# A spectral filter and a SoLU block on one core: the opening reordered, with buffers in the free half of y, idle products and conversions shared by three engines

## The chip, the core and the metric

The kernel runs on one core of a Trainium2 chip. The metric is the device time of one execution, in microseconds (us). A core has a tensor engine (PE, with its weight loads shown apart as PEld), VectorE (DVE), ScalarE (ACT), GpSimd (POOL) and SyncE (SP), which only issues transfers here. The engines run their own instruction streams and meet through semaphores. The on-chip memory is SBUF, with 128 partitions; products of PE land in PSUM.

## The reference

```python
# x (8, 3136, 256), filt_r and filt_i (1569, 256)
X = np.fft.rfft(x, axis=1)
Y = X * (filt_r + 1j * filt_i)[None]
t = np.fft.irfft(Y, n=3136, axis=1).reshape(25088, 256)
h = t @ w_in                                   # (256, 1024)
e = np.exp(h - max(h)); sm = e / (sum(e) + 1e-9)
solu = h * sm
ln = (solu - mean(solu)) / sqrt(var(solu) + 1e-6) * g_ln
out = ln @ w_out                               # (1024, 256)
```

The two weights come as 64-bit floats[...]: the kernel turns their bit patterns into 32-bit floats itself.

## The kernel before

**Two parts.** A main loop over 196 blocks of 128 tokens, taken in 98 pairs, runs the SoLU block and, interleaved with it by a table of due times (`PLAN`), the spectral filter of batches 1 to 7. Batch 0 has to be filtered before the loop can begin; this is the opening, the `with ExitStack() as st:` block from L305 on, whose order is written by hand. At its end the pools of the opening are closed and those of the main loop opened, over the same SBUF.

**The filter of one batch** is a Fourier transform in three steps. `first` (L204) multiplies pieces of x with a table (`pa`, L210), ACT copies the result to `t` (tile `t1`, L212), and it is stored to the DRAM buffer d1. x has 8 pieces of 4 columns, each with two halves of 49 rows. After all of d1 is written, 7 units (`self.units`, the last half as large) follow: `fetch` reads a unit's rows of d1 into `t2` (in the trace `t<-d`, L228), `forward` multiplies with a table `de` (`pb`, L238), `multiply` forms the complex product with the filter `f` on DVE in five operations and on POOL in one (L259 to L261), `inverse` multiplies back (`pc`) and ACT copies to `g` (L276), and `store` (L280) writes to d2. Last, `fetch_back` reads d2 into `t4` (L166, L167), and `back` makes the last products (`py`, L298), which ACT copies to `y` (L301).

**y** holds the tokens of two batches; in the opening the half of batch 1 is free and is filled at the end with six x pieces of batch 1 (`fetch_second`, L352).

**The other work of the opening:** the eight weight pieces are loaded as 32-bit words (`begin`, `load_words`, tile `raw`) and converted on DVE in ten operations of 128x512 (`load_float64`, L326 to L340); `weight_sums` forms sums of the converted w_in; tables `de` and filters `f` are loaded in two groups (units 0 and 1; the rest) by POOL, L357 and L360; the filters are copied to `f_dram` (L448) for the later batches. Ten products with an unused result (`idle`, L441) run ahead of the back transform.

**Queues.** A transfer is issued by the engine whose queue it uses, in that engine's order: SP's issues wait in front of each other, and so do POOL's and ACT's between their computations. Batch 0's fetches are on SP, the stores of `g` on POOL, the stores of `t1` on ACT (96 rows) and SP (4 rows). Completion is counted by eight semaphores for SP and ACT together and eight for POOL; a new transfer takes the next one in turn and waits until its last user has landed.

**Overlaps in SBUF.** A tile of the main loop that lies over a tile of the opening waits for that tile's last use: `h`, the first tile that the loop writes, lies over the filters `f` and so waits for their copy to f_dram.

The line numbers of the prediction and the profile before are those printed here.

Of the kernel before, what the change touches and what calls it, by code (L numbers as in the profile page):

```python
# [17 lines left out]
P = 128  # L18
# [11 lines left out]
NCH = 4  # L30
# [58 lines left out]
def kernel(  # L89
# [79 lines left out]
    class Spectrum:  # L169
# [34 lines left out]
        def first(self, i, halves, ps, evac):  # L204

            n0, n = 2 * halves[0], 2 * len(halves)
            self.t1s[i, n0] = t1 = self.pools["t1"].tile([NK, n, C], FP32,
                                                         name=f"t1_{self.e}_{i}_{n0}", tag="t1")
            for j, u in enumerate(halves):
                nc.tensor.matmul(out=ps[0:NK, j], lhsT=wf_t, rhs=self.xs[i][0:NR, 2 * u:2 * u + 2, :],  # L210
                                 start=True, stop=True)
            evac(out=t1.rearrange("p n c -> p (n c)"), in_=ps[0:NK].rearrange("p a b -> p (a b)"))  # L212
# [12 lines left out]
        def fetch(self, i, dma):  # L225
            self.t2s[i] = self.buffer(i, "t2", [P, 4, C])
            rows, n = self.rows(i, d1[self.e])
            dma(out=self.t2s[i][:, 0:n, :], in_=rows)  # L228
# [55 lines left out]
    def fetch_back(e, ch, rows_pool, split=None):  # L284

        split = split or whole
        t4s[e, ch] = rows_pool.tile([P, NCH, C], FP32, name=f"t4_{e}_{ch}", tag="r")[0:NK]
        split(
            (nc.sync.dma_start if split is by_16 else nc.gpsimd.dma_start, nc.sync.dma_start), t4s[e, ch],
            d2[e].rearrange("s (a n) c -> (s a) n c", a=4)[:, NCH * ch:NCH * ch + NCH, :])  # L290
# [14 lines left out]
    with ExitStack() as st:  # L305
        pools = {name: pool(name + "0", bufs, stack=st)
                 for name, bufs in (("r", 8), ("t1", 4), ("t2", 2), ("p", 2), ("g", 2))}
        fpool = pool("fp", 1, stack=st)
# [10 lines left out]
        def load_float64(dst, raw, negate=False):  # L319


            lo, hi = raw[:, :, 0], raw[:, :, 1]
            power = wpool.tile([P, 512], I32, name="power", tag="power", bufs=1)
            frac = dst.bitcast(I32)
            ts, stt = nc.vector.tensor_scalar, nc.vector.scalar_tensor_tensor
            ts(out=power, in0=hi, scalar1=20, scalar2=0x7FF, op0=ALU.logical_shift_right,  # L326
               op1=ALU.bitwise_and)
            ts(out=power, in0=power, scalar1=896.0, scalar2=0.0, op0=ALU.subtract, op1=ALU.max)
            ts(out=power, in0=power, scalar1=255.0, scalar2=None, op0=ALU.min)
            ts(out=power, in0=power, scalar1=23, scalar2=-2 ** 31 if negate else 0,  # L330
               op0=ALU.logical_shift_left, op1=ALU.bitwise_or)
            stt(out=power, in0=hi, scalar=-2 ** 31, in1=power, op0=ALU.bitwise_and,
                op1=ALU.bitwise_xor)
            ts(out=frac, in0=hi, scalar1=0xFFFFF, scalar2=3, op0=ALU.bitwise_and,
               op1=ALU.logical_shift_left)
            nc.vector.tensor_tensor(out=frac, in0=frac, in1=power, op=ALU.bitwise_or)
            ts(out=lo, in0=lo, scalar1=8, scalar2=None, op0=ALU.logical_shift_right)
            rest = power.bitcast(FP32)
            stt(out=rest, in0=lo, scalar=2.0 ** -44, in1=rest, op0=ALU.mult, op1=ALU.mult)
            nc.vector.tensor_tensor(out=dst, in0=dst, in1=rest, op=ALU.add)  # L340
# [7 lines left out]

        def fetch_second():
            for i in range(6):  # L350
                out = spare[i % 2][:, i // 2 * NCH * C:(i // 2 + 1) * NCH * C]
                second.fetch_x(i, [lambda out, in_: nc.sync.dma_start(out=out, in_=in_)] * 2,  # L352
                               out.rearrange("p (n c) -> p n c", c=C))

        def load_tables(i0, n):
            de = fpool.tile([P, n, 2, 2, NQ], FP32, name=f"de_{i0}", tag=f"de{i0}")
            nc.gpsimd.dma_start(out=de, in_=de_dram[i0:i0 + n].rearrange("i p k u q -> p i (k u q)"))  # L357
            f = fpool.tile([P, n, 2, C], FP32, name=f"f_{i0}", tag=f"f{i0}")
            for place, k, held, rows in all_filter_rows(i0, n):
                nc.gpsimd.dma_start(out=f[place, 0:held, k, :], in_=rows)  # L360
# [31 lines left out]
        def fetch_x(i):  # L392
            sp.fetch_x(i, (lambda out, in_: by_16((nc.sync.dma_start, nc.sync.dma_start), out, in_),
                           lambda out, in_: nc.gpsimd.dma_start(out=out, in_=in_)))
# [3 lines left out]
        pieces = NH // NCH  # L398
        for i in range(pieces):
            fetch_x(i)  # L400
            if i == 5:
                begin(0)
        begin(1)
        load_tables(0, 4)
        begin(2)
        for i in range(pieces):
            sp.first(i, (0, 1), ps_h.tile([P, 2, 512], FP32, name=f"pa_0_{i}", tag="h"),
                     nc.scalar.copy)
            sp.store_first(i, 0, lambda out, in_: by_16((nc.scalar.dma_start, nc.sync.dma_start), out, in_))
        for j in range(4):  # L410
            load_float64(weights[j][0], raws.pop(j), negate=True)
            if j == 0:
                begin(3)
                load_tables(4, NP - 4)
        nc.gpsimd.dma_start(out=wi_t, in_=wi_dram)
        nc.gpsimd.dma_start(out=g_sb, in_=moe_g_ln.rearrange("(k p) -> p k", p=P))
        weight_sums(w_in_sb)
# [6 lines left out]
        units = len(sp.units)  # L424
        for i in range(2):
            sp.fetch(i, nc.sync.dma_start)
            start(i)
        for i in range(units):
            if i + 2 < units:
                sp.fetch(i + 2, nc.sync.dma_start)  # L430
                start(i + 2)
            sp.multiply(i, 0, nc.vector.tensor_tensor)
            sp.multiply(i, 1, nc.gpsimd.tensor_tensor)
            sp.inverse(i, [ps_t.tile([P, 2, C], FP32, name=f"pc_0_{i}_{u}", tag="t") for u in range(2)])
            sp.store(i, nc.gpsimd.dma_start)
            if i in (2, 3, 4):
                begin(i + 2)

        for j in range(10):
            idle = ps_h.tile([P, 2, 512], FP32, name=f"idle_{j}", tag="h")  # L440
            nc.tensor.matmul(out=idle[:, 0, :], lhsT=tables[0][0][:, 0, 0].rearrange("p u q -> p (u q)"),  # L441
                             rhs=filters[0][0][:, 0].rearrange("p k c -> p (k c)"), start=True, stop=True)
        for ch in range(pieces):
            fetch_back(0, ch, pools["r"], by_16)
        fetch_second()
        for i0, n, rows in ((0, 4, P), (4, NP - 5, P), (NP - 1, 1, NQ)):
# [4 lines left out]
        for ch in range(pieces):  # L451
            for cb in range(KD):
                back(0, ch, cb, nc.scalar.copy)
        for j in range(4, 8):
            load_float64(weights[j][0], raws.pop(j))
            if j == 4:
                begin(7)
# [12 lines left out]

    wk = pool("wk", 1)
    wk2 = pool("wk2", 2)
    upool = pool("up", 2)
    spool = pool("sp", 1)
    rs_dram = pool("rs_dram", 2, DRAM)
    hpool = pool("hp", 2)
    pools = {name: pool(name + "1", bufs)
             for name, bufs in (("r", 3), ("t1", 3), ("t2", 1), ("p", 1), ("g", 1))}
    pools.update(f=pool("fp1", 2), de=pool("de1", 2))
# [74 lines left out]
    def pair_sums(j):  # L554

        s14 = wk2.tile([P, 2, P], FP32, name=f"s14_{j}", tag="s14")
# [352 lines left out]
```

## Time and profile before

| What | Value |
|---|---|
| Time | 1733.19 us, median of 3 runs (1730.2 to 1734.39) |
| Span of the profiled execution | 1733.2 us, 30221 instructions |
| PE busy | 1624.6 us, 94% |
| DVE, ACT, POOL busy | 71%, 54%, 63% |
| Moved by DMA | 308.71 MB, mean 178 GB/s |
| First `pb` on PE | 56.46 us |
| First `py` on PE | 107.52 us |
| First `h` on ACT | 137.84 us |

The page of a profile lists each engine's busy time, the span in 40 slices, the transfer queues, the chain of work that ended last, and groups of instructions by source line. The trace also answers for a stretch of time: a table of windows with each engine's busy time, the clock that was granted to PE, the busy share of the DMA engines and the rate; a timeline, in which equal neighbours are merged (x2); and the list of who waited for whom. `DMA_DIRECT2D` on SPq, ACTq or POOL is only the issue of a transfer, not the transfer. An engine's time in a row is that of the merged group.

### The profile page before, as it was taken

What the parts mean: (1) busy time and instruction counts of PE and PEld (TensorE: products, weight loads), DVE (VectorE), ACT (ScalarE), POOL (GpSimd) and SP (SyncE); (2) the same over time, 40 slices, a digit from 0 to 9 for tenths busy, and PEclk for the clock granted to TensorE, in tenths of its full rate; (3) what the DMA queues carried; (4) which work ended last, traced back from release to release, by engine and by line L of the source; (5) the groups of instructions that cost most, each with busy time, mean ns of one, the idle gap of its engine ahead of it and who ended that gap; (6) DMA issues with size and microseconds to landing.
All of it is one profiled execution on the core that took longest, in us unless ns stands there. A gap on an engine that the chain in (4) does not pass through costs nothing.

```text
span 1733.2 us, 30221 instructions
## 1 busy us (share of the span) xinstructions
PE 1624.6 (94%) x9792; PEld 1118.7 (65%) x9792; DVE 1225.5 (71%) x2599; ACT 939.9 (54%) x1726; POOL 1087.7 (63%) x1310
## 2 busy tenths in 40 slices
PE   4487899899999999999999999999999999999996
PEld 1352356676666667676667666766777777777776
DVE  4552877667777777678776778668777777777772
ACT  2133455546655555665566455664556566656551
POOL 4214687457666576667676666757656666567673
PEclk7688899999999999999999999999999999999999
DMA  9675788766786688658765676567754454444443
GB/s 276 188 225 182 225 246 254 200 183 167 222 243 203 170 229 237 167 153 222 233 181 139 190 220 198 154 155 210 216 139 102 119 121 120 113 105 103 112 109 92
DMA packets 363247, 308.71 MB, mean 178 GB/s; under 512 B 63425, under 2 KB 327642, under 8 KB 363090
## 3 DMA queue, kind: packets, MB, share of 16 engines
q1 hardware_dynamic: 285906, 146.01, 33.3%
q0 software_dynamic: 43984, 126.02, 24.5%
q10 hardware_dynamic: 33200, 34.74, 6.8%
q8 instruction: 80, 1.31, 0.3%
q14 instruction: 77, 0.63, 0.1%
HBM read 122.34 MB, written 81.50 MB: 118 GB/s over the span
## 4 chain that ended last, share of the span: by engine, by line
PE 71%; DMA 8%; DVE 7%; issue 3%; ACT 2%; POOL 2%; SPq 1%; ACTq 0%; POOLq 0%; DVEq 0%
PE o L686 29%; PE m L574 28%; PE py L298 5%; PE pa L210 4%; DVE h L622 3%; DMA solu_t<-turn 3%; PE pb L238 2%; PE pc L238 2%; DMA t<-d 2%; DMA de<-de_tbl 1%; ACT e L606 1%; DMA f_dram<-f 1%; DMA out_dram<-ot 1%; DVE h L595 1%; SPq L644 1%
## 5 line engine op out<-in xcount | busy, mean ns | idle before, releaser
L624 ACT ACTIVATE e<-h,nmu 128x1024 f32<-128x1024 f32 x196 | 225.3, 1150 | 338.3 <-DVE h L622 334.0
L686 PE MATMUL o<-w_out_sb,solu_t 128*128 128x128 f32 x3136 | 404.0, 277 | 4.7 <-DVE rsum L617 2.1
L686 PEld LDWEIGHTS o<-w_out_sb,solu_t 128*128 128x128 f32 x3136 | 381.6, 194 | 36.7 <-issue 29.0
L686 PEld LDWEIGHTS o<-w_out_sb,u 128*128 128x128 f32 x2352 | 307.4, 192 | 145.0 <-issue 113.3
L574 PE MATMUL m<-w_in_sb,s 128*128 128x512 f32 x784 | 397.9, 599 | 1.0 <-ACT h L584 1.0
L686 PE MATMUL o<-w_out_sb,u 128*128 128x128 f32 x2352 | 313.4, 276 | 6.4 <-ACT ot L698 5.7
L552 POOL TENSOR_TENSOR u<-solu_t 128x512 f32<-128x512 f32 x98 | 150.1, 1532 | 268.2 <-DMA solu_t<-turn 136.4
L574 PE MATMUL m<-w_in_sb,y 128*128 128x512 f32 x588 | 307.5, 606 | 7.8 <-DVE nmax L598 4.6
L622 DVE SCALAR_TENSOR_TENSOR h<-e,rsum,h 128x1024 f32<-128x1024 f32 x196 | 283.7, 1447 | 7.0
L705 DVE SCALAR_TENSOR_TENSOR ot<-o,rs_t,ot 128x128 f32<-128x128 f32 x294 | 102.6, 349 | 249.4 <-ACT ot L698 203.3
L584 ACT COPY h<-m 128x512 f32<-128x512 f32 x294 | 172.5, 587 | 132.8 <-PE m L574 113.6
L632 DVE STREAM_TRANSPOSE turn<-h 128x1024 f32<-128x1024 f32 x196 | 242.5, 1237 | 1.6 <-DVE ot L705 0.4
L598 DVE CUSTOM_DVE_ANT_0 h<-m,h 128x512 f32<-128x512 f32 x196 | 134.5, 686 | 135.4 <-ACT h L584 105.9
L606 ACT ACTIVATE e<-h,nmax 128x1024 f32<-128x1024 f32 x196 | 225.0, 1148 | 0.0
L552 POOL TENSOR_TENSOR u<-solu_t,u 128x512 f32<-128x512 f32 x98 | 139.0, 1418 | 96.6 <-PE o L686 92.7
L574 PEld LDWEIGHTS m<-w_in_sb,s 128*128 128x128 f32 x784 | 130.7, 192 | 85.3 <-issue 78.7
L298 PEld LDWEIGHTS py<-wi_t,t 100*128 100x128 f32 x1024 | 130.4, 193 | 45.5 <-issue 37.2
L552 POOL TENSOR_TENSOR solu_t<-solu_t,solu_t 128x512 f32<-128x512 f32 x98 | 147.6, 1506 | 7.7
L574 PEld LDWEIGHTS m<-w_in_sb,y 128*128 128x128 f32 x588 | 98.8, 193 | 82.9 <-issue 49.7
L301 ACT COPY y<-py 128x392 f32<-128x392 f32 x128 | 107.9, 843 | 70.0 <-PE py L298 68.6
L210 PE MATMUL pa<-x,wf_t 98*100 98x512 f32 x232 | 126.5, 638 | 19.4 <-ACT t L212 10.6
L212 ACT COPY t<-pa 100x512 f32<-100x512 f32 (+1 forms) x120 | 73.6, 614 | 122.3 <-PE pa L210 94.7
(88 smaller groups left out, 1967.0 us busy)
## 6 DMA issues: line engine op xcount, KB each, us to landing
solu_t<-turn SPq DMA_DIRECT2D x784, 128.0 KB
out_dram<-ot SPq DMA_DIRECT2D x196, 128.0 KB
d<-g POOLq DMA_DIRECT2D x45, 512.0 KB, 5.7
d<-t POOLq DMA_DIRECT2D x112, 200.0 KB, 4.6
t<-d POOLq DMA_DIRECT2D x56, 400.0 KB, 5.1
x<-in_x_dram POOLq DMA_DIRECT2D x108, 196.0 KB, 5.4
f<-f_dram POOLq DMA_DIRECT2D x39, 512.0 KB, 6.3
t<-d ACTq DMA_DIRECT2D x36, 512.0 KB
```

The source lines that it names most:

```text
L210: nc.tensor.matmul(out=ps[0:NK, j], lhsT=wf_t, rhs=self.xs[i][0:NR, 2 * u:2 * u + 2, :], start=True, stop=True)
L298: nc.tensor.matmul(out=psv[:, i:2 * NCH - i:2 * NCH - 1 - 2 * i, :], lhsT=t4s[e, ch][:, i, cb * P:cb * P + P], rhs=wi_t, start=True, stop= ...
L301: evac(out=y[:, cb, t0:t0 + S].rearrange("p (r m j) -> p m j r", m=N2 // NCH, j=NCH)[:, ch:last + 1 - ch:last - 2 * ch], in_=psv.rearrange ...
L552: nc.gpsimd.tensor_tensor(out=out, in0=in0, in1=in1, op=op)
L574: nc.tensor.matmul(out=ms[j, bank], lhsT=lhsT, rhs=w_in_sb[:, w, :], start=m in (1, 2, 7), stop=True, skip_group_check=True)
L584: nc.scalar.copy(out=h_half(k, i), in_=ms[j, 0])
L598: nc.vector.tensor_tensor_reduce(out=h_half(k, i), in0=ms[j, bank], in1=h_half(*kept), scale=1.0, scalar=sofar, op0=ALU.add, op1=ALU.min, ...
L606: nc.scalar.activation(out=e, in_=hs[k], func=AFT.Exp, bias=nmaxs.pop(k)[:, 1:2], scale=-1.0, accum_out=esum)
L622: nc.vector.scalar_tensor_tensor(out=solu, in0=e, scalar=rsum, in1=solu, op0=ALU.mult, op1=ALU.mult, accum_out=nmu)
L624: nc.scalar.activation(out=e, in_=solu, func=AFT.Square, bias=nmu, scale=-float(DFF), accum_out=variances[g][:, i:i + 1])
L632: nc.vector.transpose(out=turns[g][:, :, i, :], in_=solus.pop(k).rearrange("p (f j) -> p f j", j=32))
L686: nc.tensor.matmul(out=pos[p, bank], lhsT=lhs[:, f, :], rhs=w[:, f, :], start=f == 0 and m in (1, 2, 7), stop=True, skip_group_check=True)
```

## The change

The change touches the opening and the order in which pools are opened. It is meant to bring what is needed first in first, to fill times in which engines stand idle, and to remove waits for buffers:

- **x:** one tile for all 32 columns; transfers of 4 to 8 columns instead of 4; 48 rows and a single transfer of row 48 in place of 45 and 4.
- **Order:** all of x, raw 0 and 1 and the first tables are issued first; the other tables go in three groups instead of two, on SP between the fetches of the units; `wi_t` and `g_sb` after unit 0.
- **Buffers in y's free half:** `t1` of pieces 2 to 7, then `t2` of units 1 to 6, so that all fetches of d1 are issued at once.
- **Stores of g** move from POOL to ACT.
- **Idle products:** 8 ahead of the units, one in each unit, 7 in place of 10 ahead of the back transform.
- **Conversions:** eight operations on DVE, one scaling on ACT, two products on POOL, instead of ten on DVE; 0 and 1 before the units, 2 to 7 after them (four before and four after in the kernel before). The last chunks of the back transform's copies on ACT stand between the scalings.
- **Pools:** the filters lie lowest, under the main loop's `turn`, `ot` and `f` tiles; `s14` moves to another pool; in the main loop `t1`, `t2`, `ones` and others lie over the opening's `raw` words.

```diff
-        def fetch(self, i, dma):
-            self.t2s[i] = self.buffer(i, "t2", [P, 4, C])
+        def fetch(self, i, dma, out=None):
+            self.t2s[i] = self.buffer(i, "t2", [P, 4, C]) if out is None else out
...
+        fpool = pool("fp", 1, stack=st)
         pools = {name: pool(name + "0", bufs, stack=st)
-                 for name, bufs in (("r", 8), ("t1", 4), ("t2", 2), ("p", 2), ("g", 2))}
-        fpool = pool("fp", 1, stack=st)
+                 for name, bufs in (("t1", 2), ("r", 1), ("t2", 2), ("p", 2), ("g", 2))}
...
-            power = wpool.tile([P, 512], I32, name="power", tag="power", bufs=1)
+            power = wpool.tile([P, 512], I32, name="power", tag="power", bufs=2)
             frac = dst.bitcast(I32)
             ts, stt = nc.vector.tensor_scalar, nc.vector.scalar_tensor_tensor
+            ts(out=lo, in0=lo, scalar1=8, scalar2=None, op0=ALU.logical_shift_right)
+            rest = lo.bitcast(FP32)
+            nc.scalar.mul(rest, lo, 2.0 ** -44)
...
-            ts(out=lo, in0=lo, scalar1=8, scalar2=None, op0=ALU.logical_shift_right)
-            rest = power.bitcast(FP32)
-            stt(out=rest, in0=lo, scalar=2.0 ** -44, in1=rest, op0=ALU.mult, op1=ALU.mult)
-            nc.vector.tensor_tensor(out=dst, in0=dst, in1=rest, op=ALU.add)
+            nc.gpsimd.tensor_tensor(out=rest, in0=rest, in1=power.bitcast(FP32), op=ALU.mult)
+            nc.gpsimd.tensor_tensor(out=dst, in0=dst, in1=rest, op=ALU.add)
...
+        fetch_x(0, 0, NCH, 0, N1 - 1, nc.sync.dma_start)
+        fetch_x(0, 0, NH, N1 - 1, 1, nc.sync.dma_start)
+        for n0, n in ((NCH, NCH), (2 * NCH, 2 * NCH), (4 * NCH, 2 * NCH), (6 * NCH, 2 * NCH)):
+            fetch_x(0, n0, n, 0, N1 - 1, nc.sync.dma_start)
+        for n0, n in ((0, NCH), (NCH, NCH), (2 * NCH, 2 * NCH), (4 * NCH, 2 * NCH), (6 * NCH, 2 * NCH)):
+            fetch_x(1, n0, n, 0, N1, nc.gpsimd.dma_start)
+        for j in range(2):
+            begin(j)
+        load_tables(0, 4, nc.gpsimd.dma_start)
         for i in range(pieces):
-            fetch_x(i)
-            if i == 5:
-                begin(0)
-        begin(1)
-        load_tables(0, 4)
-        begin(2)
-        for i in range(pieces):
+            sp.xs[i] = rows_x[:, NCH * i:NCH * i + NCH]
             sp.first(i, (0, 1), ps_h.tile([P, 2, 512], FP32, name=f"pa_0_{i}", tag="h"),
-                     nc.scalar.copy)
+                     nc.scalar.copy, None if i < 2 else spare_piece(i - 2)[0:NK])
...
-        for j in range(4):
-            load_float64(weights[j][0], raws.pop(j), negate=True)
-            if j == 0:
-                begin(3)
-                load_tables(4, NP - 4)
...
-        weight_sums(w_in_sb)
+        idle_row(8, "idle")
...
+        for j in range(2):
+            convert(j)
...
+        for i in range(units):
+            sp.fetch(i, nc.sync.dma_start, spare_piece(i - 1) if i >= 1 else None)
+            if i in (2, 4):
+                load_tables(2 * i, 4 if i == 2 else NP - 8, nc.sync.dma_start)
         for i in range(2):
-            sp.fetch(i, nc.sync.dma_start)
             start(i)
         for i in range(units):
             if i + 2 < units:
-                sp.fetch(i + 2, nc.sync.dma_start)
                 start(i + 2)
             sp.multiply(i, 0, nc.vector.tensor_tensor)
             sp.multiply(i, 1, nc.gpsimd.tensor_tensor)
-            sp.inverse(i, [ps_t.tile([P, 2, C], FP32, name=f"pc_0_{i}_{u}", tag="t") for u in range(2)])
-            sp.store(i, nc.gpsimd.dma_start)
-            if i in (2, 3, 4):
-                begin(i + 2)
...
+            pss = [ps_t.tile([P, 2, C], FP32, name=f"pc_0_{i}_{u}", tag="t") for u in range(2)]
+            idle(pss[0])
+            sp.inverse(i, pss)
+            sp.store(i, nc.scalar.dma_start)
+            if i == 0:
+                nc.gpsimd.dma_start(out=wi_t, in_=wi_dram)
+                nc.gpsimd.dma_start(out=g_sb, in_=moe_g_ln.rearrange("(k p) -> p k", p=P))
+            elif i in (1, 3, 4):
+                begin({1: 2, 3: 3, 4: 4}[i])
+        idle_row(7, "idler")
...
-        for ch in range(pieces):
-            for cb in range(KD):
-                back(0, ch, cb, nc.scalar.copy)
-        for j in range(4, 8):
-            load_float64(weights[j][0], raws.pop(j))
+        for j in range(2, 8):
+            convert(j)
+            if j < 5:
+                begin(j + 3)
             if j == 4:
-                begin(7)
+                weight_sums(w_in_sb)
+            if j > 2:
+                for ch in {3: (0, 1), 4: (2, 3), 5: (4, 5), 6: (6, 7), 7: ()}[j]:
+                    for cb in range(KD):
+                        back(0, ch, cb, nc.scalar.copy)
...
-    wk = pool("wk", 1)
-    wk2 = pool("wk2", 2)
-    upool = pool("up", 2)
+    wk2 = pool("wk2", 2)
+    pools = dict(f=pool("fp1", 2))
+    upool = pool("up", 2)
+    hpool = pool("hp", 2)
+    wk = pool("wk", 1)
```

## The prediction

> **What bounds the kernel now.** I read the page first: the tensor engine (PE) is busy 94% of 1733.2 us, but in its 40 slices of 43.3 us the first two show 4 tenths, the third 8, nearly all others 8 or 9. The change touches only what runs before the main loop, so the next view is the table of windows of 10 us (columns: window, busy us of PE, weight loads, VectorE (DVE), ScalarE (ACT), GpSimd (POOL), granted clock, DMA share, GB/s):
>
> ```profile
> 10.00:20.00 10.00, 10.00 (x22) 3.59 (x20) 1.27 (x3) 4.05 (x4) 3.45 (x6) 1.00 1.04 256
> 20.00:30.00 10.00, 2.10 (x5) 0.58 (x4) 9.06 (x18) 0.00 (x0) 3.54 (x6) 0.77 1.00 312
> 30.00:40.00 10.00, 3.74 (x4) 0.99 (x4) 4.75 (x11) 4.05 (x4) 5.37 (x8) 0.50 1.01 328
> 40.00:50.00 10.00, 0.00 (x0) 0.00 (x0) 8.22 (x15) 0.00 (x0) 2.07 (x3) 0.50 1.04 294
> 80.00:90.00 10.00, 7.13 (x26) 2.95 (x24) 6.21 (x12) 2.15 (x4) 4.83 (x6) 0.50 0.48 170
> 130.00:140.00 10.00, 1.03 (x2) 0.47 (x3) 1.54 (x8) 1.07 (x2) 0.68 (x2) 0.56 0.43 159
> ```
>
> Until 50 us the DMA engines are full and PE stands still: the transfers bound that stretch. Later they are half idle, and PE waits and runs at half clock. The timeline gives the borders (start, length, engine, line; in brackets the idle time before and its releaser):
>
> ```profile
> 46.27 25.19 SPq L228 DMA_DIRECT2D t<-d  x7
> 56.46 3.44 PE L238 MATMUL pb<-t,de 64*64 64x256 f32 x32 [20.00 <-DMA t<-d]
> 66.95 0.78 POOL L280 DMA_DIRECT2D d<-g  x1 [3.84 <-ACT g L276]
> 98.09 0.32 SPq L166 DMA_DIRECT2D t<-d  x1
> 107.52 16.36 PE L298 MATMUL py<-wi_t,t 100*128 100x98 f32 x128
> 137.84 0.58 ACT L584 COPY h<-m 128x512 f32<-128x512 f32 x1 [13.09 <-DMA f_dram<-f]
> 138.32 0.59 ACT L212 COPY t<-pa 100x512 f32<-100x512 f32 x1
> ```
>
> Four stages: A to 46.3 us (x in, first transform, d1 stored), B to 98.1 (the seven units), C to 123.9 (back transform), D to 137.8, where ACT's first h waits for the store of the filters, because h lies over their tile. I take 138.3 us, ACT's first `t<-pa` of the second batch, as the main loop's start; what moves it moves the end, since from there PE is nearly full and its order does not change.
>
> [...]a conversion meets a GpSimd product:
>
> ```profile
> 89.68 1.51 POOL L261 TENSOR_TENSOR pi<-pi,pt 128x512 f32<-128x512 f32 x1
> 90.11 1.63 DVE L332 SCALAR_TENSOR_TENSOR power<-raw,power 128x512 int32<-128x512 int32 x1
> 92.72 0.42 DVE L337 TENSOR_SCALAR raw<-raw 128x512 int32<-128x512 int32 x1
> 93.17 0.69 DVE L339 SCALAR_TENSOR_TENSOR power<-raw,power 128x512 f32<-128x512 int32 x1
> ```
>
> L332 takes 0.69 elsewhere; here it ends 0.55 us after the POOL product, as if it had waited for it. [...]the ten idle products start at 97.31 with pieces of 0.85 us and have 0.43 us from 100.65. [...]A lone 512 KB `t<-d` takes 4.1 us here (unit 2's, which waits for unit 0's products, at about 58.2, and is used at 62.30).
>
> **The change, part by part.**
> Stage A. All x goes first, then raw 0 and 1, then tables 0 to 3; tables 4 to 12 and raws 2, 3 leave stage A. Before d1 is complete must move: x 3.2 MB, two raws 1.05, tables 1.6, d1 3.3, together 9.1 MB. The kernel before moved 12.6 MB by 46.3 us (the windows summed), from about 3 us on: 291 GB/s. So 9.1 MB take 31 us: d1 complete at 34. PE does not bind: 8 pieces at 1.75 from 7 us end at 21. Eight new idle products then wait for filter tile 0 (31 to 34) and, cold after ten idle us, take 3.4 + 6 x 0.86 = 8.6: until about 41. pb of unit 0 follows, where it was at 56.46: 15 us gained.
>
> Stage B. All seven units have their own buffer, so their fetches wait for no unit, but they share the SP queue with tables 4 to 12. The eight completion semaphores of the SP and ACT queues rotate: in the built program the third filter load of the last table waits for the store of unit 0's result, and behind it on SP stand the other loads and the fetches of units 5 and 6. Unit 0: three pb of 1.6 from 41, idle product 0.9, pc 1.2 with the POOL product, two g copies 1.07: stored at 49, landed at 54 (d<-g lands in 5.7). The filter load lands at 59, unit 5's fetch at 63, pb 1.6, DVE for units 5 and 6 3.05 + 2.1: DVE ends the units at 70, where it was 87.3. POOL no longer stands in the ring of a unit: ACT issues the stores, where POOL waited for g and issued (0.76) before its next product. The pace by engines alone would so be 4 us a unit (pb 1.6, idle 0.9, pc 1.2 on PE; DVE 3.1) instead of 4.6 to 6.5, and 41 + 7 x 4 = 69: both ways lead to the same time. The idle product in each unit holds the clock at 1.0 where it fell to 0.50.
>
> Stage C. Store of unit 6 at 72; t4 arrives 9.4 later as before (98.1 to 107.5): 81. PE and ACT need 16.4: 98 if nothing else held them. But six conversions now stand on DVE behind the units, where four did. Each had ten DVE operations, 5.4 us. It now has eight: six of 0.46, two of 0.61, 4.0 us; ACT's scaling 0.6 (nearest: its copies of 128x512, 0.587) is hidden in idle ACT; POOL gets two products of 1.27, 2.5 us. [...]So 6.5 a conversion is the upper value, 4.0 the lower; the rows above make me take 6.5. Six: 39; the sums of w_in 2.6; pair_sums(0) on POOL, between conversions 6 and 7, 1.8: 43.5, from 70 to 113.5. The y copies of the last chunks stand behind the scaling of raw 6 on ACT (100) and end at 103, before that.
>
> Stage D. The filters now lie under turn and ot, first written three steps later, so the 13 us wait goes. In its place ACT's first `t<-pa` waits for conversion 7, whose words lie under t1; h on DVE stands behind it; PE's next products and POOL's d1 stores wait for that copy. Main loop from 114 instead of 138.3: 24 gained.
>
> After that. f_dram and the second x are 3.2 + 2.4 MB behind t4, raws 5 to 7 and two x pieces: 11.3 MB from 76.5, at the 242 GB/s of 98 to 138, to 123. Filters are first read 26 us into the loop (140), so no wait, but the d1 stores run beside it: up to 3 us. Against it, POOL has issued the last two x pieces before the loop, where they stood ahead of the first d1 store (138.37 to 141.41, 3 us). I set these off. Later steps have the same instructions and as many buffers: nothing. 1733 - 24 = 1709.
>
> **The rivals.**
> R1[...]: conversions at 4.0 to 4.5 give 70 + 27 + 4.4 = 101; then transfers bound: all but f_dram is 28 MB, at 291 GB/s 97 us, from 3: 100. Start at 101, and less hiding of f_dram's stores (3): 34 gained, 1699. For it: during 61.84 to 63.1 POOL's product runs and DVE's 0.68 stay 0.68; against: those read PSUM and one SBUF tensor, which is not the case at hand.
> R2, stage B is starved: a fetch under full queues took 10.2 us (46.27 to 56.46) instead of 4.1, and the semaphores couple loads and stores. Then d1 at 38, pb at 48, unit 0's store landed at 66, unit 5 at 78, DVE at 87; conversions[...] (L330 took 1.44 once) 8 each, 48 + 4.4: 139.5, with f_dram beside the first steps 3 more: 4 lost, 1737, slower. For it: SP's waits; against: fewer bytes are in flight than at 46 us.
> R3, half of R2: 124, gain 14, 1719.
>
> **How the numbers follow.** Main case 0.52: 1709 (1704 to 1714 for stage B by 5 us). R1 0.24: 1699. R3 0.14: 1719 to 1727. R2 0.10, of which 0.06 slower by over 0.3% (above 1738), 0.04 within. Faster 0.90, same 0.05, slower 0.05 after rounding. The range from R1's 1699 less 4 for stage A at 320 GB/s, to R3's far end: 1695 to 1724.
>
> **What would show it.** Right: first pb near 41, DVE's last unit product near 70, conversion operations on DVE of 0.43 stretched above 1 us wherever POOL multiplies, no wait of h for f_dram, the first `t<-pa` of batch two near 114 with DVE busy throughout from 70, and the rest of the span as long as before (1595). Wrong: conversions of 4 us (R1); SP idle before unit 5 beyond 65 (R2, R3); or a longer loop.

## The result, and the profile after

The changed kernel takes 1724.05 us (median of 4 executions, 1719.4 to 1726.56) against 1733.51: a ratio of 0.9946, with a 95% interval of 0.992 to 0.9972. A second measurement gave 0.9941 (0.9925 to 0.9957). It is faster by 9.5 us, not by the 24 that were predicted, and 1724.05 lies just outside the range.

First the table of windows of the changed kernel, for the same stretches as before (columns: window, busy us of PE, weight loads, DVE, ACT, POOL, granted clock, DMA share, GB/s):

```profile
10.00:20.00 10.00, 7.47 (x8) 1.97 (x8) 0.00 (x0) 2.02 (x2) 1.14 (x2) 1.00 1.03 185
20.00:30.00 10.00, 9.39 (x15) 3.49 (x16) 2.39 (x6) 3.04 (x3) 2.74 (x5) 1.00 1.01 322
30.00:40.00 10.00, 6.51 (x13) 2.27 (x12) 5.05 (x11) 4.25 (x5) 4.28 (x5) 0.83 0.71 252
40.00:50.00 10.00, 9.94 (x52) 4.39 (x55) 0.85 (x2) 0.00 (x0) 1.45 (x2) 0.82 0.93 281
80.00:90.00 10.00, 8.57 (x49) 3.60 (x47) 9.76 (x19) 3.89 (x7) 4.00 (x4) 1.00 0.57 191
130.00:140.00 10.00, 6.63 (x14) 1.98 (x13) 0.43 (x1) 3.86 (x7) 2.84 (x6) 0.95 0.54 197
```

From 130 to 140 us PE has work where it stood still; from 40 to 50 it is busy too, but until 48 with the idle products, whose result nobody uses. And from 10 to 20 us the DMA engines are as full as before and move 185 GB/s, where the kernel before moved 256. Then the rows of the timeline that answer to the borders of the stages, and those that explain them:

```profile
37.47 10.54 PE L428 MATMUL idle<-f,de 128*128 128x512 f32 x16 [3.43 <-DMA f<-in_filt_i_dram]
40.10 0.41 SPq L229 DMA_DIRECT2D t<-d  x1
47.94 1.11 PE L239 MATMUL pb<-t,de 64*64 64x256 f32 x16
51.10 10.94 SPq L366 DMA_DIRECT2D f<-in_filt_r_dram  x4
55.97 0.40 ACTq L281 DMA_DIRECT2D d<-g  x1
72.35 2.01 PE L239 MATMUL pb<-y,de 64*64 64x256 f32 x16 [10.18 <-DVE pi L260]
92.94 8.25 PE L300 MATMUL py<-wi_t,t 100*128 100x98 f32 x64 [0.47 <-DMA t<-d]
107.09 10.56 PE L300 MATMUL py<-wi_t,t 100*128 100x98 f32 x48 [2.56 <-ACT y L303]
119.44 0.58 ACT L619 COPY h<-m 128x512 f32<-128x512 f32 x1 [0.43 <-PE m L609]
124.39 1.07 ACT L213 COPY t<-pa 100x512 f32<-100x512 f32 x2 [4.37 <-POOL w_out_sb L343]
131.91 0.58 ACT L213 COPY t<-pa 100x512 f32<-100x512 f32 x1 [4.60 <-DMA d<-t]
```

The wait of the first h is gone. The main loop starts at 124.39 instead of 138.32, with the end of the last conversion (the releaser is GpSimd's product of L343), as forecast, but 10 us late. One row was not in the forecast at all: the back transform `py` does its first 64 products in 8.25 us and the last 48 in 10.56, at half clock (1.00 granted from 77.66 to 104.96, then 0.50 to 122.03). Another was there only as a loss of up to 3 us that something else would make good: the main loop's fourth copy waits 4.60 us for a d1 store.

| | predicted | measured |
|---|---|---|
| d1 complete (first fetch on SP) | 34 | 40.10 |
| first `pb` | 41 | 47.94 |
| unit 5's `pb` | 63 | 72.35 |
| DVE ends the units | 70 | 83.67 |
| first `py`, last `py` | 81, 98 | 92.94, 117.64 |
| last conversion | 113.5 | 124.36 |
| main loop's start | 114 | 124.39 |
| from there to the first e (the first exponential of the SoLU block, on ACT) | 29.2 | 31.43 |

### The profile page after: what moved, and what is told of

It is laid out like the page before. It is cut to its first block, busy times and chain, and to the rows that moved or that the text cites. A ratio compares the mean times of both kernels' runs of the same rounds, so it can differ in the third digit from the quotient of the medians.

```text
span 1717.6 us, 30283 instructions
## 1 busy us (share of the span) xinstructions
PE 1635.2 (95%) x9816; PEld 1120.8 (65%) x9816; DVE 1219.0 (71%) x2583; ACT 945.1 (55%) x1734; POOL 1095.7 (64%) x1307
## 4 chain that ended last, share of the span: by engine, by line
PE 77%; DMA 9%; DVE 7%; ACT 2%; issue 2%; POOL 2%; SPq 1%; ACTq 0%; DVEq 0%; POOLq 0%
PE o L721 31%; PE m L609 30%; PE pa L211 5%; PE py L300 5%; PE pb L239 3%; DMA de<-de_tbl 3%; PE pc L239 2%; DVE h L657 2%; DMA t<-d 2%; DMA solu_t<-turn 1%; DMA d<-t 1%; DVE turn L667 1%; DMA y<-in_x_dram 1%; DMA f<-in_filt_i_dram 1%; DVE pt L261 1%
## 5 line engine op out<-in xcount | busy, mean ns | idle before, releaser
L721 PEld LDWEIGHTS o<-w_out_sb,solu_t 128*128 128x128 f32 x3136 | 379.7, 193 | 35.3 <-issue 28.3
L633 DVE CUSTOM_DVE_ANT_0 h<-m,h 128x512 f32<-128x512 f32 x196 | 134.5, 686 | 111.6 <-ACT h L619 82.1
L587 POOL TENSOR_TENSOR u<-solu_t,u 128x512 f32<-128x512 f32 x98 | 139.8, 1427 | 93.4 <-PE o L721 89.4
L300 PEld LDWEIGHTS py<-wi_t,t 100*128 100x128 f32 x1024 | 135.8, 200 | 50.8 <-issue 39.4
L300 PE MATMUL py<-wi_t,t 100*128 100x98 f32 x1024 | 137.8, 282 | 12.9 <-DMA t<-d 8.8
L211 PE MATMUL pa<-x,wf_t 98*100 98x512 f32 x232 | 129.0, 651 | 13.1 <-DMA x<-in_x_dram 13.1
```

The lines of the kernel that those rows point to most:

```text
L300: nc.tensor.matmul(out=psv[:, i:2 * NCH - i:2 * NCH - 1 - 2 * i, :], lhsT=t4s[e, ch][:, i, cb * P:cb * P + P], rhs=wi_t, start=True, stop= ...
L587: nc.gpsimd.tensor_tensor(out=out, in0=in0, in1=in1, op=op)
L633: nc.vector.tensor_tensor_reduce(out=h_half(k, i), in0=ms[j, bank], in1=h_half(*kept), scale=1.0, scalar=sofar, op0=ALU.add, op1=ALU.min, ...
L721: nc.tensor.matmul(out=pos[p, bank], lhsT=lhs[:, f, :], rhs=w[:, f, :], start=f == 0 and m in (1, 2, 7), stop=True, skip_group_check=True)
```

## The experiments

Single executions of one kernel spread over 5 to 16 us, so the times below are medians of interleaved runs, each with the ratio to the kernel before. They come from four comparisons, in which the kernel before had medians of 1733.51 (first two rows), 1731.56 (runs 1 to 4), 1731.92 (5 to 8) and 1731.35 us (9 to 11 and the repeat), so rows are compared by their ratios; an interval of a ratio is some 0.001 to 0.003 to either side. The points in the opening come from one profile of each kernel. From the first e to the end these profiles take 1558 to 1570 us, without a pattern by kernel: a gain of 2 us in the opening can't be seen in one execution.

| kernel | median, ratio | DVE ends units | py | start | first e |
|---|---|---|---|---|---|
| before | 1733.51 | 87.35 | 107.5–123.9 | 138.3 | 167.5 |
| changed | 1724.05, 0.9946 | 83.67 | 92.9–117.6 | 124.4 | 155.8 |
| changed, again | 1721.54, 0.9941 | 85.42 | 94.3–119.4 | 126.2 | 157.7 |
| 1 before + pools | 1725.73, 0.9969 | 86.41 | 107.8–124.3 | 127.3 | 161.8 |
| 2 x as before | 1721.59, 0.9939 | 81.81 | 90.5–115.8 | 122.5 | 153.9 |
| 3 stores on POOL | 1724.44, 0.9949 | 75.75 | 91.1–119.5 | 125.0 | 154.8 |
| 4 conversions on DVE | 1723.72, 0.9946 | 85.26 | 94.1–122.1 | 125.8 | 158.0 |
| 5 filters copied early | 1719.48, 0.9930 | 88.47 | 97.1–122.5 | 129.7 | 156.4 |
| 6 = 3 and 4 | 1722.66, 0.9954 | 77.55 | 93.4–119.7 | 124.1 | 155.1 |
| 7 = 6, 11 idle | 1722.64, 0.9957 | 78.27 | 96.8–120.7 | 125.0 | 156.3 |
| 8 combined | 1715.08, 0.9904 | 79.26 | 92.2–117.2 | 122.1 | 147.1 |
| 9 = 8, 16 idle | 1710.12, 0.9879 | 78.44 | 95.3–111.9 | 116.3 | 144.2 |
| 10 = 8, x behind t4 | 1704.83, 0.9842 | 72.37 | 93.7–110.2 | 113.1 | 141.4 |
| 11 before + pools + 5 | 1716.13, 0.9917 | 87.63 | 108.4–124.8 | 127.9 | 154.7 |

**1. The order of pools alone.**

```diff
-                 for name, bufs in (("r", 8), ("t1", 4), ("t2", 2), ("p", 2), ("g", 2))}
-        fpool = pool("fp", 1, stack=st)
+        fpool = pool("fp", 1, stack=st)
+                 for name, bufs in (("t1", 4), ("r", 8), ("t2", 2), ("p", 2), ("g", 2))}
...
-    wk = pool("wk", 1)
-    wk2 = pool("wk2", 2)
-    upool = pool("up", 2)
+    wk2 = pool("wk2", 2)
+    pools = dict(f=pool("fp1", 2))
+    upool = pool("up", 2)
+    hpool = pool("hp", 2)
+    wk = pool("wk", 1)
...
```

> The kernel before with the new order of pools alone (filters lowest, s14 moved; transfers, units and conversions as before). Theory: in the changed kernel the last conversion ends at 124.4 us and in the kernel before at 123.9, so nearly all of the 9.5 us gained is the removed wait of the first h for the copy of the filters (13.09 us), and reordering stages A to C gave nothing at the start of the main loop. Then here the first t<-pa of batch 2 comes at 125 to 126 us instead of 138.3 and the time is 1720 to 1725 us, within 3 us of the changed kernel. Rival: the copy of the filters (3.2 MB), now beside the first d1 stores, takes the wait's place; then under 5 us are gained here (1729 or more), and the 9.5 us of the changed kernel come from stages A to C.

The ratio is 0.9969 (0.9959 to 0.9978): 5.8 us of gain. ACT and SP in its timeline:

```profile
124.66 8.92 SPq L448 DMA_DIRECT2D f_dram<-f  x3
125.42 0.58 ACT L585 COPY h<-m 128x512 f32<-128x512 f32 x1 [0.31 <-PE m L575]
127.30 0.58 ACT L212 COPY t<-pa 100x512 f32<-100x512 f32 x1 [1.30 <-PE pa L210]
136.71 0.58 ACT L212 COPY t<-pa 100x512 f32<-100x512 f32 x1 [6.95 <-DMA d<-t]
```

The main loop starts 11.0 us earlier, but 5.4 of it are lost before the first e (34.5 us instead of 29.2): the copies of the filters run from 124.66 on, beside the first d1 stores, and ACT waits 6.95 us for one. Theory and rival are each half right: the wait of h that is gone (13.1 us) is nearly as large as the changed kernel's whole gain at the start (13.9), and half of what it gives here comes back as another wait. Stages A to C, which the prediction credited with 10 us, gave the changed kernel 1 to 3 us at its start (124.4 and 126.2 against 127.3).

**2. x fetched as before.**

```diff
-        fetch_x(0, 0, NCH, 0, N1 - 1, nc.sync.dma_start)
-        fetch_x(0, 0, NH, N1 - 1, 1, nc.sync.dma_start)
...
+        for i in range(pieces):
+            fetch_x(0, NCH * i, NCH, 0, 45, nc.sync.dma_start)
+            fetch_x(0, NCH * i, NCH, 45, 4, nc.sync.dma_start)
+            fetch_x(1, NCH * i, NCH, 0, N1, nc.gpsimd.dma_start)
```

> The changed kernel with x fetched as in the kernel before: pieces of 4 columns each, 45 and 4 rows, into the one tile. Theory: the larger transfers of x (8 KB packets of 710 ns where 4 KB ones take 250 to 280) are why 5 to 20 us moved only 176 to 195 GB/s and d1 was complete at 40 instead of 34. Then here the first pa starts below 8.5 us, d1's first fetch is issued at 34 to 36, pb of unit 0 starts near 43 to 44, and, if nothing else holds the units, the units end 4 us earlier and the main loop starts at 120: 4 us faster. Rival: the sum of bytes and the small packets bind, whatever the pieces: first fetch at 39 to 41 as in the changed kernel, no gain. A third way: d1 is earlier, but units 5 and 6 still wait for their filters and unit 5's fetch behind the store, so that the units end within 1.5 us of 83.6 and the time is the same.

PE and SP in its timeline:

```profile
7.81 15.00 PE L211 MATMUL pa<-x,wf_t 98*100 98x512 f32 x28 [7.81 <-DMA x<-in_x_dram]
35.70 0.41 SPq L229 DMA_DIRECT2D t<-d  x1
```

The first pa starts 2.9 us earlier and PE no longer waits for x after it; d1 is complete at 35.70 instead of 40.10, `pb` comes at 44.91 instead of 47.94. So the new way of fetching x cost 4.4 of the 6 us by which d1 was late; the edit undoes the wider pieces and the other split of the rows together, and doesn't tell them apart. At the main loop's start 1.9 are left; the median doesn't tell it from the changed kernel.

**3. Stores of g on GpSimd again.**

```diff
-            sp.store(i, nc.scalar.dma_start)
+            sp.store(i, nc.gpsimd.dma_start)
```

> The changed kernel with the stores of g issued by GpSimd again. The last group's filter loads on SP then share no semaphore with a store. Theory: it was this coupling that held unit 5's filters and fetch (SP idle 10.9 us from 51.1), so unit 5's pb comes at 64 to 67 us instead of 72.35, the units end at 77 to 79 on DVE instead of 83.6, and the main loop starts 4 to 6 us earlier: 1718 to 1720 us. Rival: between 50 and 70 us the DMA engines are full (290 to 310 GB/s) and the loads could not have landed earlier; then unit 5 comes at 70 or later, GpSimd's wait for g stands in the ring again, and the units end at 83 or later: same or up to 4 us slower.

SP and PE in its timeline:

```profile
50.92 2.94 SPq L366 DMA_DIRECT2D f<-in_filt_r_dram  x4
59.56 1.16 SPq L229 DMA_DIRECT2D y<-d  x2
65.98 1.12 PE L239 MATMUL pb<-y,de 64*64 64x256 f32 x16 [0.90 <-DMA y<-d]
```

The same four filter loads of L366 that took SP 10.94 us take 2.94, unit 5's `pb` comes 6.4 us earlier and DVE ends the units 7.9 earlier. The coupling by the shared semaphores was real: in the changed kernel the third of these loads waits 8.0 us for unit 0's store, which holds the same semaphore. Yet the main loop starts at 124.95 and the time is the same. GpSimd's ring is back, so the last store of g is issued at 84.96, only 1.8 us earlier, and py, at half clock again (its last 112 products take 23.91 us), ends at 119.5; and the conversions wait for raw words and for their scalings, which stand on ACT between py's copies, and end at 124.9. Neither theory had this.

**4. Conversions on DVE alone.**

```diff
...
-            nc.scalar.mul(rest, lo, 2.0 ** -44)
...
-            nc.gpsimd.tensor_tensor(out=rest, in0=rest, in1=power.bitcast(FP32), op=ALU.mult)
-            nc.gpsimd.tensor_tensor(out=dst, in0=dst, in1=rest, op=ALU.add)
+            stt(out=rest, in0=lo, scalar=2.0 ** -44, in1=rest, op0=ALU.mult, op1=ALU.mult)
+            nc.vector.tensor_tensor(out=dst, in0=dst, in1=rest, op=ALU.add)
...
```

> The changed kernel with each conversion as in the kernel before: ten operations on DVE, none on ScalarE and GpSimd. Theory[...]: GpSimd's two products a conversion (1.35 each) stop DVE, so sharing cost more than it took off: six conversions at 5.4 and 4.4 of sums take 36.8 us instead of 40.8, the last ends at 120.4 instead of 124.4, and the kernel is 3 to 5 us faster, 1720. Rival: what stretches DVE's operations is their own form or the transfers, not GpSimd; then DVE has 1.4 us more to do in each, 6 x 1.4 = 8 us later, and the kernel is 6 to 9 us slower, 1731.

First a conversion beside GpSimd's two products in the changed kernel's timeline, then DVE and PE in that of the experiment:

```profile
93.14 1.35 POOL L342 TENSOR_TENSOR raw<-raw,power 128x512 f32<-128x512 f32 x1 [1.09 <-issue]
93.38 1.66 DVE L341 TENSOR_TENSOR w_in_sb<-w_in_sb,power 128x512 int32<-128x512 int32 x1
95.19 1.34 POOL L343 TENSOR_TENSOR w_in_sb<-w_in_sb,raw 128x512 f32<-128x512 f32 x1 [0.16 <-DVE w_in_sb L341]
95.30 1.52 DVE L331 TENSOR_SCALAR power<-raw 128x512 int32<-128x512 int32 x1
```

```profile
88.48 0.69 DVE L338 TENSOR_TENSOR w_in_sb<-w_in_sb,power 128x512 int32<-128x512 int32 x1
101.31 20.77 PE L300 MATMUL py<-wi_t,t 100*128 100x98 f32 x96 [3.09 <-DMA t<-d]
121.87 3.03 PE L608 MATMUL m<-w_in_sb,y 128*128 128x512 f32 x4
```

DVE's operations of 0.69 and 0.42 take 1.66 and 1.52 where GpSimd multiplies, and end 0.55 and 0.29 us after its product, as if they had waited for it; without GpSimd's products no operation of these six conversions takes more than 0.83. From DVE's last unit operation to the last conversion it is 36.5 us instead of 40.7, with two operations more on DVE in each. As to DVE the theory stands: GpSimd's products did hold it up. Still nothing is gained: py ends at 122.1, at half clock (96 products in 20.77 us) after a wait for t4, and now holds the main loop's start (125.80).

**5. Filters copied before t4 is fetched.** The loop of four `f_dram` copies is moved ahead of `fetch_back`.

> The changed kernel with the four copies of the filters to f_dram issued on SP ahead of the fetches of t4 instead of behind the second x. Theory: at 120 to 126 us these 3.2 MB run beside the first d1 stores of batch 2; from the start of the main loop (124.39) to the first e (155.82) the changed kernel takes 31.4 us where the kernel before, with the copies over, took 29.2. Moved to 67 us, into the stretch in which the DMA engines are a third busy (70 to 80: share 0.34), they cost nothing: main loop's start as in the changed kernel, 29 to 29.5 us from there to the first e, 2 to 3 us faster. Rival: they push back the last stores of g, the raw words and t4, so that py starts after 96 instead of 92.94 and the main loop's start moves by as much: same or 2 us slower.

The window of 70 to 80 us, in the changed kernel and in this one:

```profile
70.00:80.00 10.00, 7.32 (x44) 3.07 (x48) 4.46 (x7) 1.07 (x2) 2.00 (x2) 0.62 0.34 109
```

```profile
70.00:80.00 10.00, 3.02 (x18) 1.46 (x18) 3.27 (x5) 0.00 (x0) 1.30 (x2) 0.50 1.05 357
```

Both are right in part: from start to first e it takes 26.7 us instead of 31.4, but the units still had loads and stores to come in that window, and end 4.8 us later. In sum the first e is where it was; the median is 1719.48, ratio 0.9930 (0.9904 to 0.9955).

**6 and 7. Both chains of stage C.** Number 6 makes the edits of 3 and 4 together; 7 has 11 idle products ahead of py instead of 7.

```diff
-        idle_row(7, "idler")
+        idle_row(11, "idler")
```

> The changed kernel with both: stores of g on GpSimd and conversions on DVE alone. Each alone gave no shorter time, though the first ended the units on DVE at 75.75 instead of 83.6, and the second took the six conversions and sums from 40.8 to 36.6 us. Theory: stage C has two chains of nearly equal length, the conversions and the back transform on PE, which runs at half clock (py x112 in 23.9 us); shorten the conversions and the back transform sets the start. Then here the last conversion ends at 112 to 114, py ends at 119 to 121 and the main loop starts at 122 to 124: no more than 2 us faster than the changed kernel. Rival, the prediction's account: the conversions alone set the start; then it is at 114 to 116 and the time is 8 to 10 us shorter, near 1714.

> As the run before, with 11 idle products instead of 7 ahead of the back transform, so that py starts 3.6 us later, when more of t4 has landed. Theory: waits of PE of 2.5 to 3.4 us between the first chunks (for t4) made the clock fall to half for the 17 to 27 us of py; without these waits py runs at full clock, 128 products in about 16.4 us as in the kernel before: py from 95 to 112, main loop from 115 to 117, 6 us faster than without the four idle products. Rival: the clock falls anyway (the products of 98 columns, or the pace of ACT's copies); then py ends 3 us later, at 123, and the main loop starts at 125 or later.

PE in the timeline of 6, then of 7:

```profile
93.40 2.00 PE L300 MATMUL py<-wi_t,t 100*128 100x98 f32 x16 [0.56 <-DMA t<-d]
95.99 2.00 PE L300 MATMUL py<-wi_t,t 100*128 100x98 f32 x16 [0.58 <-DMA t<-d]
98.94 20.81 PE L300 MATMUL py<-wi_t,t 100*128 100x98 f32 x96 [0.95 <-ACT y L303]
```

```profile
96.84 6.08 PE L300 MATMUL py<-wi_t,t 100*128 100x98 f32 x48
103.24 2.00 PE L300 MATMUL py<-wi_t,t 100*128 100x98 f32 x16 [0.32 <-DMA t<-d]
106.71 14.02 PE L300 MATMUL py<-wi_t,t 100*128 100x98 f32 x64 [1.48 <-DMA t<-d]
```

Number 6 starts the main loop at 124.12, close to its theory: DVE ends the units 6.1 us and the conversions 5.7 us earlier than in the changed kernel (they end at 118.7, later than expected, for a late raw), and py holds the start. Number 7 missed: the four products were too few, two waits for t4 were left, and the clock fell again (0.50 from 110 to 120 us).

**8, 9 and 10. All together, and py without waits.** Number 8 takes the edits of 2, 4 and 5, issues tables 4 to 12 on GpSimd (in place of 3), and has 11 idle products. Number 9 has 16. Number 10 has 14, a third buffer for g, and the last two x pieces of batch 2 on SP behind t4. Of these edits the fence shows the tables and the x pieces:

```diff
-                load_tables(2 * i, 4 if i == 2 else NP - 8, nc.sync.dma_start)
+                load_tables(2 * i, 4 if i == 2 else NP - 8, nc.gpsimd.dma_start)
...
-                    i, [lambda out, in_: nc.gpsimd.dma_start(out=out, in_=in_)] * 2)))
+                    i, [lambda out, in_, sp=sp: (nc.sync if sp.e == 1 else nc.gpsimd).dma_start(
+                        out=out, in_=in_)] * 2)))
...
```

> What the runs point to, in one: the changed kernel with x fetched as before, tables 4 to 12 issued by GpSimd ahead of the units (stores of g stay on ACT), conversions on DVE alone, 11 idle products ahead of the back transform, copies of the filters ahead of t4. If the shares add up: pb of unit 0 at 44 to 45, units end on DVE at 74 to 77, conversions at 112 to 114, py over at 110 to 112, main loop from 114, first e at 143, and the time 10 us below the changed kernel: 1712 to 1715. If the DMA engines are the bound of stage B (tables beside the fetches of d1): pb of unit 0 at 50 or later and the units end at 82 or later, the main loop from 120, and the time within 3 us of the changed kernel.

> The combined kernel with 16 idle products instead of 11 ahead of the back transform: py starts 4.3 us later, at 96.5, when its chunks have landed. Theory: in the combined kernel, and in the changed one, two or three waits of PE of 2 us between chunks (for t4, at 98 to 107 us) let the clock fall to half from 104.6 on, and the rest of py and the first products of the main loop take double. Without the waits py runs at 16.4 us, ends at 113 and not at 117, the four m after it take 2.0 and not 3.7, and the main loop starts at 116 to 118 instead of 122.1, though py began later: 4 to 5 us faster than the combined kernel. Rival: the clock falls anyway, py ends at 121 or later, main loop from 126, 4 us slower.

> The combined kernel with 14 idle products, a third buffer for g (ScalarE waited 4.4 us at 65 to 70 for one to be stored), and the last two x pieces of batch 2 (0.8 MB) on SP behind the other six, instead of on GpSimd beside t4. If t4 is held up by what lands beside it, its chunks come 2 to 3 us earlier, units end on DVE at 75 to 77 instead of 79.3, py runs from 92 to 109 at full clock, conversions end at 112 to 113, and the main loop starts at 113 to 114: 8 us faster than the combined kernel, near 1707. If not: as in the run with 16 idle products, near 1711.

PE and ACT in the timeline of 9, then of 10:

```profile
81.45 14.00 PE L425 MATMUL idler<-f,de 128*128 128x512 f32 x32
95.28 16.59 PE L300 MATMUL py<-wi_t,t 100*128 100x98 f32 x128
111.93 2.04 PE L606 MATMUL m<-w_in_sb,y 128*128 128x512 f32 x4
116.27 0.58 ACT L213 COPY t<-pa 100x512 f32<-100x512 f32 x1 [2.60 <-DVE w_out_sb L342]
```

```profile
93.65 16.51 PE L300 MATMUL py<-wi_t,t 100*128 100x98 f32 x128
113.10 0.59 ACT L213 COPY t<-pa 100x512 f32<-100x512 f32 x1 [1.19 <-PE pa L211]
```

Number 8 met neither account: its py fell to half clock like the others (0.50 from 105 to 120 us) and its start is at 122.1, but its copies of the filters were over, and it has the first e after 25.0 us: 1715.08. In 9, with five idle products more and nothing else changed, py starts 3.1 us later and ends 5.3 earlier, the m after it take 2.04 instead of 3.67, and the main loop starts 5.8 us earlier, now held by the conversions. The ratios of 8 and 9 overlap (0.9877 to 0.9931, 0.9858 to 0.9900), but the granted clock, averaged over each whole execution, sets them apart: 0.982 to 0.988 in the six executions of 9, 0.975 to 0.982 in those of 8. In 10 the start is at 113.10, by three edits whose shares no run tells apart. With 1704.83 us, 0.9842 (0.9825 to 0.9858), it is clearly faster than both kernels (the changed one had 0.9941, 0.9925 to 0.9957, in the same comparison).

**11. The kernel before with two edits.** Number 1, with the copies moved as in 5.

> The kernel before with two edits: the new order of pools and the copies of the filters ahead of the fetches of t4; transfers, units, idle products and conversions as before. Theory: the wait of h (13 us) and what took its place, the copies beside the first d1 stores (34.5 us from the main loop's start to the first e instead of 29.2), are both gone: start at 125 to 127, first e at 152 to 154, and 1716 to 1720 us, less than the changed kernel's 1723, without any of its reordering of stages A to C. Rival: the copies delay the last units' stores and t4 by the 11 us that their 3.2 MB take; then py starts at 112 to 118, the main loop at 131 to 136, and the time is 1723 or more.

SP, ACT and PE in its timeline:

```profile
72.11 3.45 SPq L445 DMA_DIRECT2D f_dram<-f  x3
108.41 16.38 PE L298 MATMUL py<-wi_t,t 100*128 100x98 f32 x128
127.86 0.59 ACT L212 COPY t<-pa 100x512 f32<-100x512 f32 x1 [1.32 <-PE pa L210]
```

In the old order the copies hurt nothing (py starts within 1 us of where it did), the first e comes 26.8 us after the start, and the ratio is 0.9917 (0.9902 to 0.9932): 1716.13 us against 1721.54 for the changed kernel in the same comparison. With four and six executions, and intervals that overlap, this says that the two edits do at least as well as the changed kernel; that they do better is likely and not shown.

> The changed kernel once more, unaltered, on the chip of the three others, to compare them with it directly: main loop's start at 124 to 126, first e 31 to 32 us later, 1721 to 1726 us, and half clock from about 105 us to the end of the back transform.

This repeat of the changed kernel met its expectation (start at 126.15, first e 31.6 us later, half clock from 103.6 to 124.0, which is 5 us beyond the end of the back transform).

## Why the prediction was wrong

**Right:** the wait of h is gone; the last conversion sets the main loop's start; GpSimd's products stretch DVE's operations (1.66 and 1.52 us beside them, at most 0.83 without them in run 4), and six conversions with their sums took 40.7 us where 43.5 were forecast, the first only 4.4, with GpSimd's first product of a conversion at its very end (87.95). The 6.5 us for each were an estimate from the one meeting in the kernel before; that none of DVE's eight operations runs beside a product was not shown there. From the start to the end it takes 1593 and 1595 us in the two profiles, 1595 before.

**Stage A, "291 GB/s".** The bytes were right (9.2 MB by 40 us), the rate was not. This mean was taken from a stretch with many kinds of transfers and applied to one in which, at first, only x moves. Between 5 and 20 us the changed kernel moved 176 to 195 GB/s at a full DMA share. So the third piece of x is there at 20.61 us only, where all eight pieces were to be through by 21:

```profile
20.61 13.43 PE L211 MATMUL pa<-x,wf_t 98*100 98x512 f32 x24 [1.90 <-DMA x<-in_x_dram]
```

Behind it the first transform, which was said not to bind, takes 13.43 us for six pieces, and the last store some 5 more: d1 was 6.1 us late, 4.4 of it by the way x is fetched (run 2). The idle products began at 37.47, when the last filter of the first tables had landed (some 32.4 forecast), and took 10.54 us instead of 8.6; PE goes from them to the first `pb` without a gap, 6.9 us late.

**Stage B, "DVE ends the units at 70".** The coupling of loads and stores was seen, and its cost put too low. Unit 0's store was to land at 54 and release the third filter load; that load was issued at 61.26, late by little more than stage A. But the loads then took longer, and the standstill behind them had a second price:

```profile
61.26 0.31 SPq L366 DMA_DIRECT2D f<-in_filt_r_dram  x1
70.27 0.69 DVE L261 TENSOR_TENSOR pt<-pb,f 128x512 f32<-128x512 f32 x1 [4.46 <-DMA f<-in_filt_i_dram]
74.29 2.07 PE L428 MATMUL pc<-f,de 128*128 128x512 f32 x2
78.09 0.69 DVE L260 TENSOR_TENSOR pr<-pb,f 128x512 f32<-128x512 f32 x1 [5.21 <-PE pc L239]
```

The filters that DVE needed had landed 9.0 us after the release, where 5 had been put. Meanwhile PE's clock had fallen to half (67.4 to 77.7 us), although "the idle product in each unit holds the clock at 1.0": the idle product stands in PE's order behind the waiting `pb`, then takes 2.07 us itself (the row of L428) instead of 0.9, and DVE waits 5.21 us for the products behind it. From the first `pb` to unit 5's it took 24.4 us (22 forecast), and from there to DVE's last unit operation 11.3 (7 forecast); together 35.7 where 29 had been put, and without the coupling 28.9 (run 3).

These are the steps that failed for the changed kernel: 6.9 and 6.7 us late at the end of the units, less 2.8 us at the conversions, make 10.8 us at the last conversion and 10.4 at the start. Mending one of them moved the time by little, for a step that the changed kernel's own last wait doesn't show:

**Stage C, "PE and ACT need 16.4".** This came from a row in which all of t4 arrived in time. Here it arrives while raw words and x pieces are loaded, PE waits between chunks, the clock falls to half (from 104.96 on), and py takes 24.7. In the changed kernel it stays hidden by some 3 us (the m after it ends at 121.1, the last conversion at 124.4); as soon as the conversions are shorter, it holds the start (runs 4, 6, 7, 8). Run 9 shows it by idle products alone, and run 10, with all these steps mended, starts at 113.1. That 114 had been forecast is no confirmation: its conversions, on DVE alone, end at 107.6 and not at 113.5, and py, which ends at 110.2 and not at 98, sets its start.

**After the start, "I set these off".** The copies of the filters beside the first d1 stores were put at up to 3 us and balanced against x pieces issued earlier. Measured: 2.3 us lost up to the first e in the changed kernel, 5.4 in run 1; with the copies earlier, 25.0 to 28.3 us (runs 5, 8 to 11), which is 0.9 to 4.2 better than the kernel before.

24 less 10.4 less 2.3 leaves 11.3; the medians say 9.5 and 9.8, whose intervals hold it. The third rival named the start (124) and the time (1719 to 1727), and part of that is luck: "half of R2" was a mean of two cases, not a chain of its own. Stages A and B came out nearly as the second rival had them (first `pb` at 48, units until 87), the conversions nearly as the main case did. 0.14 was too little for a case that needed only stages A and B to be late.

**Left open:** whether the 8 idle products at the front are worth their 10 us, and what the larger pieces of x are slowed by; no run tried either. That the idle products held back the first `pb` is likely: in the packet records of the changed kernel as many bytes as unit 0's fetch has (0.52 MB) had moved on that queue by 43.3 us, and `pb` came at 47.94.

## What to carry to other kernels

Where two chains run side by side, work out both with the state that they will be in (arriving data, granted clock), not with the row of a kernel in which one of them had no waits; the chain that is hidden today holds the gain tomorrow. A removed wait is worth what is left after its cause has found another place: move the transfer that caused it into a stretch where it delays nothing before counting the wait as gained. Here two edits, which put tiles and one copy elsewhere, did at least as well as the whole reordering.

## What the runs showed of the hardware

- **Larger pieces of x were slower, and not by their packets alone.** In the trace's packet records between 5 and 15 us, x in pieces of 8 columns comes in packets of 8 KB, 710 ns each in the mean (11.5 GB/s on one engine); in the kernel before they are of 4 KB and 256 to 308 ns (13 to 16 GB/s). But packets of 4 KB were slow too at times: 339 to 371 ns on GpSimd's queue beside those of 8 KB, and 354 to 361 ns in run 2 from 10 to 15 us. The cause isn't shown.
- **Short gaps between narrow products halved the clock, and it did not recover under them.** Every record of the granted clock in these traces, but for the last one, which the end of the program cuts off, lasts a multiple of 3.41 us; so it can be asked what PE did in each such stretch. Run 6 (columns as in the tables of windows):

```profile
92.30:95.71 3.41, 2.54 (x18) 1.86 (x16) 3.27 (x7) 1.13 (x2) 2.77 (x4) 1.00 0.88 232
95.71:99.12 3.41, 2.18 (x18) 2.08 (x18) 3.34 (x6) 2.25 (x3) 1.54 (x2) 1.00 0.97 234
99.12:102.53 3.41, 3.41 (x18) 3.41 (x17) 3.24 (x8) 0.87 (x2) 0.00 (x0) 0.50 1.05 283
119.60:123.01 3.41, 3.41 (x6) 1.25 (x6) 0.00 (x0) 1.40 (x2) 1.73 (x4) 0.50 0.77 291
123.01:126.42 3.41, 3.37 (x9) 1.06 (x8) 3.10 (x16) 1.52 (x3) 0.91 (x2) 1.00 1.05 401
```

  With 0.87 us of idle time of PE in a stretch the clock held; after 1.23 us in the next, no single gap longer than 0.95, it was halved. In all nine profiles in which py had to wait it fell at the end of the first stretch with 1.1 to 2.6 us of idle time, and up to 0.87 us were without effect; in the five in which py ran without waits (the kernel before and runs 1, 9, 10 and 11) it stayed at 1.00 throughout py. The sum alone is not the rule: between the products of the units 1.88 us in one stretch did not halve it (run 6, 78.6 to 82.1).

  Under the idle products, of 512 columns, it did recover: in the kernel before they began at 97.31, and the record of full clock begins at 100.42; in the changed kernel at 37.47 and 43.52. Under py it didn't: in run 6 py ran for 20.8 us without a gap, nearly all of it at half clock, and full clock came back only after the stretch from 119.60 on, of which all but the first 0.15 us belonged to the products of m and pa, of 512 columns. It was the same in the other eight (in run 4 py still had 1.4 us of that stretch). Why these products of 98 columns hold a full clock but don't bring it back is not shown.
